# A rewritten end for a top-k attention and mixture-of-depths kernel: order, PSUM tiles, engines and the last scatter

## Chip, cores and metric

The kernel runs on one core of a Trainium2 chip. The metric is the device time of one execution in microseconds (us); lower is better. A core has five engines that the profile names PE (TensorE, matmuls; PEld is its weight load), DVE (VectorE), ACT (ScalarE), POOL (GpSimd) and SP (SyncE, here a queue of transfers). Each works through its own instructions in order and waits on semaphores for the others.

## The reference

Two blocks follow each other: top-k attention, then a mixture of depths over the result.

```python
# attention: q, k, v are (8, 8, 576, 64)
scores = scale * np.matmul(q, k.transpose(0, 1, 3, 2))
kth = np.partition(scores, -32, axis=-1)[..., -32:-31]
scores = np.where(scores >= kth, scores, -1000000000.0)
attn = softmax(scores)                       # written out in the reference
x = attn @ v                                 # -> (8, 576, 512), heads side by side
# mixture of depths: w_gate (512), w1 (512, 1024), w2 (1024, 512), capacity 128
gate = np.einsum('bsd,d->bs', x, w_gate)
out = x.copy()
for b in range(8):
    top_idx = np.argpartition(-gate[b], 128)[:128]
    xe = x[b, top_idx]
    ye = np.maximum(xe @ w1, 0.0) @ w2
    out[b, top_idx] = xe + sigmoid(gate[b, top_idx])[:, None] * ye
```

## The kernel before

A batch of 576 rows is cut into four tiles of 128 rows and a last one of 64 (`J` = 4, `NT` = 5). A unit is a tile with two heads; the last tile puts four heads in one unit. That gives 18 units a batch and N = 144 in all. One software pipeline runs over the units. A unit goes through these steps:

- `multiply` and `keep`: scores on PE into the PSUM tile `ps`, copied to SBUF as `sc` by ACT.
- `find_bound` (DVE): a bound on the kth score from maxima of seven parts.
- `what_is_below`: ACT takes the sign of score against bound (`sides`, two instructions, with a sum in `seen`), POOL multiplies score and sign into `y`.
- `kth_of` (DVE): the eight largest of `y` (`next`), the last of which is the kth score.
- `mask_of`: `less` is 1 in bf16 where a score lies below the kth. In the loop ACT takes one half and POOL the other.
- `weigh`: PE turns the scores (`turn`, `turn_last`) and adds a large negative number where `less` is set; ACT takes the exponential into `pT` and `last`.
- `values` (PE) multiplies with v into `av`; `keep_values` (ACT) copies to `xs`, `keep_sums` keeps the denominators `sums`.
- When a tile is whole, `normalise` divides (`rden` on DVE, the product `x` on POOL), and `gates` takes the dot product with w_gate on DVE (`gate`).

When a batch is whole its rows are stored from `x` by SP, and `mixture` follows in slices between the units of the next batch: each gate is counted against all others (`junk`, with the count in `rank`), the rank is compared with the slot numbers (`pick`), PE multiplies `pick` with the split parts of row number and gate (`parts`, made by `split` on POOL), an indirect transfer on POOL gathers the 128 rows `xe`, PE turns them (`xeT`), multiplies with w1 (`h_ps`, `hT`) and w2 (`y_ps`), and POOL scatters the product `gy`, adding to the rows in `out`.

All engine instructions go through `InOrder`, which keeps them in program order, so the order of the text is the order on each engine, and the profile gives line 45 for nearly all of them. [...] `ps_sc` takes four (the score tile `ps`), `ps_tr` two (`ptr`), `ps_av` one (`av`), `ps_misc` one.

After the loop (from line 1188) the end of the last batch is written out. Units N-4 to N-1 are still to be weighed. They take turns between the tiles `ptr`, `av` and, by `other_room`, the score tile, both halves of which carry the name `ps`. `closing`, a generator, holds the selection of the last batch without a trip through DRAM: `spread` turns the gates into a row on all partitions, `count` counts, `split`, five `pick`, places, gather, the multiplications, and one scatter that writes x + g y. Slices of `between`, the mixture of batch B-2, are put into it. A certificate follows: DVE reduces `least`, `seen`, `sums`, `ranks` and `others` to one flag `unsure`, and `count_unsure` puts it through PE. All engines load the flag (line 1298), and an exact general path would run if it were set.

Of the kernel before, what the change touches and what calls it, by code (L numbers as in the profile page):

```python
# [10 lines left out]
AF = mybir.ActivationFunctionType  # L11
# [8 lines left out]
CAP = 128  # L20
# [11 lines left out]
J = 4  # L32
# [16 lines left out]
def kernel(  # L49
# [38 lines left out]
        tc.tile_pool(name="dram", bufs=2, space=bass.MemoryType.DRAM)  # L88
    )
    PS = bass.MemoryType.PSUM  # L90
    ps_sc = ctx.enter_context(tc.tile_pool(name="ps_sc", bufs=1, space=PS))
    ps_tr = ctx.enter_context(tc.tile_pool(name="ps_tr", bufs=1, space=PS))
    ps_av = ctx.enter_context(tc.tile_pool(name="ps_av", bufs=1, space=PS))
    ps_misc = ctx.enter_context(tc.tile_pool(name="ps_misc", bufs=1, space=PS))


    ident = const.tile([P, P], FP32, name="ident")
# [48 lines left out]
    ranks = const.tile([P, B, NT], FP32, name="ranks")  # L146
    nc.gpsimd.memset(ranks, 0.0)

    others = const.tile([P, J], FP32, name="others")

# [34 lines left out]
    def flush():  # L187
        while late:
            late.pop(0)()
# [5 lines left out]
    def flush_pool():  # L195
        while pool_late:
            pool_late.pop(0)()
# [545 lines left out]
        )  # L743
        pool_late.append(lambda: add_rows(gy, row_i))

    def closing(b, pg, between):

        gate, rank = pg[0], ranks[:, b, :]
        gate_row = modpool.tile([P, S], FP32, name="gate_row")
        pick = modpool.tile([P, NT, CAP], BF16, name="pick")

        def spread(t0, t1):
            tr = ps_tr.tile([P, 2, J, P], FP32, name="ptr")
            n = R if t0 == J else P
            for t in range(t0, t1):
                pe.transpose(  # L760
                    tr[:, 0, t - t0, 0:n],
                    gate[0:n, t : t + 1].to_broadcast([n, P]),
                    ident[0:n, 0:n],
                )
            act.copy(
                out=gate_row[:, t0 * P : (t1 - 1) * P + n].rearrange(
                    "p (t i) -> p t i", i=n
                ),
                in_=tr[:, 0, 0 : t1 - t0, 0:n],
            )  # L770

        def count(t, among, rank):
            n = R if t == J else P
            junk = modpool.tile([P, S], FP32, name="junk", tag="scratch")
            dve.tensor_scalar(
                out=junk[0:n, among],
                in0=gate_row[0:n, among],
                scalar1=gate[0:n, t : t + 1],
                scalar2=None,
                op0=ALU.is_gt,  # L780
                op1=ALU.add,
                accum_out=rank[0:n, t : t + 1],
            )

        spread(0, J)
        yield
        for t in range(J):
            count(t, slice(0, JP), rank)
            if t == 1:
                yield  # L790
        yield
        spread(J, NT)
        split(*pg)
        for _ in range(2):
            next(between)
        for t in range(J):
            count(t, slice(JP, S), others)
        for t in range(J):
            (pool if t < 3 else dve).tensor_scalar(
                out=pick[:, t, :],  # L800
                in0=slot,
                scalar1=rank[:, t : t + 1],
                scalar2=others[:, t : t + 1],
                op0=ALU.subtract,
                op1=ALU.is_equal,
            )
        count(J, slice(0, S), rank)
        dve.tensor_scalar(
            out=pick[0:R, J, :],
            in0=slot[0:R, :],  # L810
            scalar1=rank[0:R, J:NT],
            scalar2=None,
            op0=ALU.is_equal,
        )
        ps = ps_av.tile([P, 512], FP32, name="av")[:, 0:6]
        place = stats.tile([P, 2], FP32, name="place")
        row_i = modpool.tile([P, 1], I32, name="row_i", bufs=2)
        g = modpool.tile([P, 1], FP32, name="g", bufs=2)
        multiply_places(ps, pick, pg)
        add_parts(place, ps)  # L820
        keep_rows(place, row_i, float(b * S), float((b + 1) * S - 1))
        xe = modpool.tile([P, HD], FP32, name="xe")
        fetch_rows(xe, out[0 : b + 1], row_i)
        dve.tensor_scalar_max(out=g, in0=place[:, 1:2], scalar1=-88.0)
        act.activation(g, g, AF.Exp, scale=-1.0)
        for _ in between:
            pass
        flush()
        flush_pool()
        yield  # L830
        dve.tensor_scalar_add(out=g, in0=g, scalar1=1.0)
        dve.reciprocal(out=g, in_=g)

        xeT = modpool.tile([P, NDC, CAP], FP32, name="xeT")
        ps = ps_tr.tile([P, 2, J, P], FP32, name="ptr")[:, 0, :, :]
        for dc in range(NDC):
            pe.transpose(ps[:, dc, :], xe[:, dc * P : (dc + 1) * P], ident)
        act.copy(out=xeT, in_=ps)
        yield
        hT = modpool.tile([P, NFC, CAP], FP32, name="hT")  # L840
        for f0 in range(0, NFC, 2):
            h_ps = (
                lambda: room_for_scores()[:, 0, 0, :],
                lambda: ps_av.tile([P, 512], FP32, name="av"),
                lambda: ps_misc.tile([P, 512], FP32, name="h_ps", tag="misc"),
                lambda: ps_tr.tile([P, 2, J, P], FP32, name="ptr")[:, 0, :, :].rearrange(
                    "p c i -> p (c i)"
                ),
            )[f0 // 2 % 4]()
            for i in range(2):  # L850
                multiply_h(h_ps[:, i * CAP : (i + 1) * CAP], f0 + i, xeT)
            act.activation(
                hT[:, f0 : f0 + 2, :],
                h_ps[:, 0 : 2 * CAP].rearrange("p (f i) -> p f i", f=2),
                AF.Relu,
            )
        ps = room_for_scores()[:, 0, 0, :]
        for fc in range(NFC):
            pe.matmul(
                ps, hT[:, fc, :], w2[:, fc, :], start=(fc == 0), stop=(fc == NFC - 1)  # L860
            )

        gy = modpool.tile([P, HD], FP32, name="gy")
        dve.scalar_tensor_tensor(
            out=gy, in0=ps, scalar=g[:, 0:1], in1=xe, op0=ALU.mult, op1=ALU.add
        )
        put_rows(gy, row_i)

    def multiply_places(ps, pick, pg):

        for t in range(NT):
            n = R if t == J else P
            pe.matmul(
                ps,
                pick[0:n, t, :],
                pg[1][0:n, t, :, :].rearrange("p a e -> p (a e)"),
                start=(t == 0),
                stop=(t == J),
            )

    def split(gate, parts):

        rest = modpool.tile([P, NT], FP32, name="rest")
        pool.tensor_copy(out=parts[:, :, 1, 0], in_=gate)
        pool.tensor_tensor(rest, gate, parts[:, :, 1, 0], ALU.subtract)
        pool.tensor_copy(out=parts[:, :, 1, 1], in_=rest)
        pool.tensor_tensor(rest, rest, parts[:, :, 1, 1], ALU.subtract)
        pool.tensor_copy(out=parts[:, :, 1, 2], in_=rest)
# [29 lines left out]

        put_rows(gy, row_i, compute_op=ALU.add)

    def put_rows(rows, row_i, **how):
        pool.indirect_dma_start(
            out=out.flatten_outer_dims(),
            out_offset=bass.IndirectOffsetOnAxis(ap=row_i, axis=0),
            in_=rows,
            in_offset=None,
            **how,
        )
# [256 lines left out]

    def other_room():
        ps = room_for_scores()
        return ps[:, 0, :, :].rearrange("p u (c i) -> p u c i", c=J), ps[:, 1, 0, :]  # L1190

    x, pg = of_batch[B - 1]
    between = mixtures[B - 2]
    last_out = out[B - 1]
    weighed = {}

    def weigh_unit(m):
        tr, av = other_room() if (N - m) % 2 else room_to_turn()
        weighed[m] = *weigh(scs.pop(m), tr, av, masks.pop(m)), av

    def values_unit(m):
# [9 lines left out]
        n = R if t == J else P  # L1211
        keep_sums(n, xs, sums[0:n, (B - 1) * NT + t, :])

    weigh_unit(N - 4)
    weighed[N - 4][2]()
    what_is_below(N - 1)
    mask_of(N - 3, (dve, dve))
    weigh_unit(N - 3)
    kth_of(N - 2)
    mask_of(N - 2, (act, dve))  # L1220
    values_unit(N - 4)
    weighed[N - 3][2]()
    keep_unit(N - 4, xs)
    flush()
    weigh_unit(N - 2)
    kth_of(N - 1)
    mask_of(N - 1, (act, dve))
    values_unit(N - 3)
    weighed[N - 2][2]()
    keep_unit(N - 3, xs)  # L1230
    sums_of(J - 1, xs)
    normalise(B - 1, J - 1, xs)
    store_full(last_out, x)
    weigh_unit(N - 1)
    gates(B - 1, J - 1)
    values_unit(N - 2)
    weighed[N - 1][2]()
    xs = xpool.tile([P, H, DE], FP32, name="xs")
    keep_unit(N - 2, xs)
    closed = closing(B - 1, pg, between)  # L1240
    next(closed)
    values_unit(N - 1)
    for _ in range(2):
        next(between)
    keep_unit(N - 1, xs)
    sums_of(J, xs)
    next(closed)
    normalise(B - 1, J, xs)
    store_last(last_out, x)
    next(closed)  # L1250
    gates(B - 1, J)
    next(closed)


    keep_least(B - 1, bounds.pop(B - 1)[:, :, :, 7], next8s.pop(B - 1)[:, :, :, 7])
    sure = stats.tile([P, 1], FP32, name="sure")
# [23 lines left out]
    dve.memset(ones, 1.0)  # L1280
    unsure = const.tile([1, 1], I32, name="unsure")

    def count_unsure():
        ps = ps_av.tile([P, 512], FP32, name="av")
        pe.matmul(ps[0:1, 0:1], sure, ones)
        dve.tensor_scalar(
            out=unsure,
            in0=ps[0:1, 0:1],
            scalar1=-1.0,
            scalar2=float(P + B * (S * (S - 1) // 2)),  # L1290
            op0=ALU.mult,
            op1=ALU.add,
        )

    next(closed)
    count_unsure()
    next(closed, None)
    is_unsure = nc.values_load(unsure[0:1, 0:1])  # L1298


    def general_weights(sc):
# [103 lines left out]
```

## Time and profile before

| | us |
|---|---|
| median of three runs | 826.69 (826.53 to 827.79) |
| the profiled execution, as run | 828.44 |
| its span in the profile | 826.1 |
| PE busy | 777.0 (94%) |
| DVE busy | 787.2 (95%) |
| ACT busy | 730.7 (88%) |
| POOL busy | 715.4 (87%) |
| mean granted clock of TensorE | 0.99 |

The span is what the profiler saw of one execution; the time as run holds some more around it. A busy share is an average over the whole span. The page also cuts the span into 40 slices of equal length and gives the busy share of each engine in tenths, a 9 standing for 90% or more. The loop over the units fills the span from the start to about 780 us; the end after the loop takes the rest. A trace answer lists single instructions with their start, and in brackets how long the engine had been idle before and which engine's instruction ended the wait.

### The profile page before, as it was taken

What the parts mean: (1) busy time and instruction counts of PE and PEld (TensorE: products, weight loads), DVE (VectorE), ACT (ScalarE), POOL (GpSimd) and SP (SyncE); (2) the same over time, 40 slices, a digit from 0 to 9 for tenths busy, and PEclk for the clock granted to TensorE, in tenths of its full rate; (3) what the DMA queues carried; (4) which work ended last, traced back from release to release, by engine and by line L of the source; (5) the groups of instructions that cost most, each with busy time, mean ns of one, the idle gap of its engine ahead of it and who ended that gap; (6) DMA issues with size and microseconds to landing.
All of it is one profiled execution on the core that took longest, in us unless ns stands there. A gap on an engine that the chain in (4) does not pass through costs nothing. (4 is left out here: it accounts for less than half of the span.)

```text
span 826.1 us, 28252 instructions
## 1 busy us (share of the span) xinstructions
PE 777.0 (94%) x10143; PEld 596.5 (72%) x10143; DVE 787.2 (95%) x4651; ACT 730.7 (88%) x1557; POOL 715.4 (87%) x722
## 2 busy tenths in 40 slices
PE   6888888888999999999999999999999999999976
PEld 5566666666887778877787777877787777767744
DVE  7899999999999999999999999999999999999960
ACT  4799999999999999999999999999999999879831
POOL 3799999999899999999899999999999998899831
PEclk9699999999999999999999999999999999999999
DMA  7931111521141221521223221512215102101021
GB/s 170 283 86 40 28 66 28 105 53 27 60 92 36 53 40 59 112 47 34 79 47 86 53 40 60 104 23 54 40 59 112 28 15 66 23 12 18 2 71 30
DMA packets 122133, 50.38 MB, mean 61 GB/s; under 512 B 116417, under 2 KB 116417, under 8 KB 120961
## 3 DMA queue, kind: packets, MB, share of 16 engines
q1 hardware_dynamic: 118672, 43.91, 22.0%
q0 software_dynamic: 1728, 4.20, 2.8%
q8 instruction: 82, 1.34, 0.8%
q14 instruction: 67, 0.54, 0.3%
q10 hardware_dynamic: 1584, 0.39, 0.2%
HBM read 36.93 MB, written 11.55 MB: 59 GB/s over the span
## 5 line engine op out<-in xcount | busy, mean ns | idle before, releaser
L45 POOL TENSOR_TENSOR y<-sc,sides 128x576 f32<-128x576 f32 x288 | 365.1, 1289 | 57.0 <-ACT sides L45 54.3
L45 DVE MAX8 cand<-sc 128x8 f32<-128x82 f32 (+1 forms) x2016 | 314.0, 228 | 2.7 <-ACT sc L45 2.7
L45 POOL TENSOR_SCALAR less<-sc,next 128x576 bf16<-128x576 f32 x135 | 232.5, 1722 | 12.9 <-DVE next L45 10.0
L45 PE MATMUL ptr<-out_of_reach,less 128*128 128x128 bf16 x1136 | 205.3, 220 | 19.5 <-POOL less L45 19.4
L45 ACT ACTIVATE sides<-sc,bound 128x576 bf16<-128x576 f32 x288 | 223.0, 787 | 0.0
L45 PE MATMUL ptr<-ident,sc 128*128 128x128 f32 x1136 | 217.0, 282 | 0.0
L45 DVE MAX8 next<-y 128x8 f32<-128x584 f32 x288 | 204.4, 751 | 1.7 <-POOL y L45 1.6
L45 PEld LDWEIGHTS av<-v,pT 128*64 128x64 f32 x4544 | 144.1, 137 | 66.9 <-ACT last L45 63.2
L45 PE MATMUL ps<-kT,qT 64*128 64x288 f32 (+1 forms) x1280 | 182.0, 431 | 5.2 <-ACT qT L45 5.2
L45 PEld LDWEIGHTS ptr<-ident,sc 128*128 128x128 f32 x1136 | 161.3, 142 | 29.1 <-issue 17.4
L45 ACT ACTIVATE pT<-ptr 128x1024 f32<-128x1024 f32 x142 | 145.3, 1023 | 33.2 <-PE ptr L45 32.2
L45 PE MATMUL av<-v,pT 128*64 128x65 f32 x4544 | 163.7, 224 | 9.3 <-ACT last L45 8.5
L45 ACT COPY sc<-ps 128x1152 f32<-128x1152 f32 (+1 forms) x144 | 162.2, 1126 | 3.5 <-PE ps L45 3.5
L45 PEld LDWEIGHTS <-less 128*128 128x128 bf16 x1296 | 136.1, 106 | 39.2 <-POOL less L45 25.2
L45 PEld LDWEIGHTS ps<-kT,qT 64*128 64x128 f32 (+1 forms) x1280 | 100.2, 178 | 41.5 <-issue 21.2
L45 ACT ACTIVATE less<-sc,next 128x576 bf16<-128x576 f32 x143 | 111.2, 777 | 12.7 <-DVE next L45 10.8
L45 DVE MATCH_REPLACE8 cand<-best,cand 128x21 f32<-128x21 f32 (+1 forms) x576 | 99.0, 180 | 0.0
L45 DVE MAX8 best<-cand 128x8 f32<-128x21 f32 (+1 forms) x576 | 90.5, 190 | 0.0
L45 PE MATMUL h_ps<-xeT,w 128*128 128x128 f32 x464 | 65.8, 286 | 0.0
L45 PEld LDWEIGHTS h_ps<-xeT,w 128*128 128x128 f32 x464 | 55.8, 191 | 9.2 <-issue 5.8
L45 PE MATMUL y_ps<-w,hT 128*128 128x512 f32 x112 | 60.6, 636 | 0.0
L45 ACT ACTIVATION_READ_ACCUMULATOR sides<-sc,bound 128x1 f32 x288 | 59.9, 208 | 0.0
(133 smaller groups left out, 866.4 us busy)
## 6 DMA issues: line engine op xcount, KB each, us to landing
v<-in_v_dram SPq DMA_DIRECT2D x64, 128.0 KB, 4.2
out_dram<-x SPq DMA_DIRECT2D x8, 1024.0 KB, 3.9
rows<-in_k_dram SPq DMA_DIRECT2D x56, 128.0 KB, 2.9
rows<-in_q_dram SPq DMA_DIRECT2D x56, 128.0 KB, 3.1
w<-in_moe_w_dram SPq DMA_DIRECT2D x2, 2048.0 KB
gate_row<-row_dram SPq DMA_DIRECT2D x7, 288.0 KB, 4.4
w<-in_k_dram SPq DMA_DIRECT2D x8, 128.0 KB, 3.2
last<-in_k_dram SPq DMA_DIRECT2D x8, 128.0 KB, 4.0
```

What stands on the lines that cost most here:

```text
L45: return lambda *a, **kw: self._tc.keep_in_program_order(fn(*a, **kw))
```

## The change

Nothing in the loop over the units changes but where its PSUM score tile lies: `ps_sc` is opened last and closed after the loop, and a pool `ps_end` takes its four banks for the end, as `tr2` (two banks), `av2` and `av3`. `closing` goes; its steps stand in the open at the end, in another order:

- The signs of the last unit come ahead of everything else of the end.
- Units N-3 and N-1 are weighed in `tr2` with `av2` and `av3`, units N-4 and N-2 in `ptr` with `av` as before.
- The masks of N-3, N-2 and N-1 are all made by DVE, with a sum that nothing reads (`compare`). Before, N-3's two were DVE's, and the other four were shared by ACT and DVE; none had a sum.
- The gates of tiles 0 to 2 are spread and counted against each other while the last units are weighed; those of tile 3 and of the last tile are counted when they are known, in columns of their own (`others`, now with five columns and cleared at the start).
- The last tile's `x` is made by DVE in place of POOL.
- The slots: tiles 0 and 1 by POOL, tile 2 by ACT as relu(1 - |rank - slot|), tiles 3 and 4 by DVE. Before: three by POOL, two by DVE.
- `xeT` is copied in two halves, by ACT and by DVE.
- The certificate's matmul stands between the two multiplications, and the flag is loaded ahead of the last steps of DVE and POOL.
- The product with w2 is made in two halves of 256 columns, each with its own `gy` and its own scatter, into `out` seen as rows of 256.

```diff
+    all_steps = ExitStack()
+    ps_sc = all_steps.enter_context(tc.tile_pool(name="ps_sc", bufs=1, space=PS))
...
-    others = const.tile([P, J], FP32, name="others")
+    others = const.tile([P, NT], FP32, name="others")
+    nc.gpsimd.memset(others, 0.0)
...
-    def closing(b, pg, between):
...
+    all_steps.close()
+    end = ExitStack()
+    ps_end = end.enter_context(tc.tile_pool(name="ps_end", bufs=1, space=PS))
...
+    def other_room(m):
+        tr = ps_end.tile([P, 2, J, P], FP32, name="tr2")
+        return tr, bank(ps_end, "av2" if m == N - 3 else "av3")
...
+    def compare(out, in0, scalar, op, total):
+        dve.tensor_scalar(
+            out=out, in0=in0, scalar1=scalar, scalar2=None,
+            op0=op, op1=ALU.add, accum_out=total,
+        )
...
+    what_is_below(N - 1)
     weigh_unit(N - 4)
+    rows_ps = bank(ps_end, "av3")
+    turn_gates(0, J - 1, rows_ps)
     weighed[N - 4][2]()
-    what_is_below(N - 1)
-    mask_of(N - 3, (dve, dve))
+    keep_gates(0, J - 1, rows_ps)
+    mask_both(N - 3)
     weigh_unit(N - 3)
     kth_of(N - 2)
-    mask_of(N - 2, (act, dve))
     values_unit(N - 4)
     weighed[N - 3][2]()
     keep_unit(N - 4, xs)
     flush()
+    mask_both(N - 2)
     weigh_unit(N - 2)
     kth_of(N - 1)
-    mask_of(N - 1, (act, dve))
     values_unit(N - 3)
     weighed[N - 2][2]()
     keep_unit(N - 3, xs)
     sums_of(J - 1, xs)
+    mask_both(N - 1)
     normalise(B - 1, J - 1, xs)
     store_full(last_out, x)
     weigh_unit(N - 1)
+    for t in range(2):
+        count(t, slice(0, (J - 1) * P), rank)
     gates(B - 1, J - 1)
+    count(2, slice(0, (J - 1) * P), rank)
     values_unit(N - 2)
     weighed[N - 1][2]()
     xs = xpool.tile([P, H, DE], FP32, name="xs")
     keep_unit(N - 2, xs)
-    closed = closing(B - 1, pg, between)
-    next(closed)
+    tr = ps_tr.tile([P, 2, J, P], FP32, name="ptr")[:, 0, 0, :]
+    turn_gates(J - 1, J, tr)
+    keep_gates(J - 1, J, tr)
     values_unit(N - 1)
     for _ in range(2):
         next(between)
     keep_unit(N - 1, xs)
     sums_of(J, xs)
-    next(closed)
-    normalise(B - 1, J, xs)
+    count(J - 1, slice(0, JP), rank)
+    rden = stats.tile([P, H], FP32, name="rden")
+    dve.reciprocal(out=rden[0:R, :], in_=sums[0:R, (B - 1) * NT + J, :])
+    dve.tensor_tensor(
+        x[0:R, J, :].rearrange("p (h d) -> p h d", h=H), xs[0:R, :, 0:D],
+        rden[0:R, :].unsqueeze(2).to_broadcast([R, H, D]), ALU.mult,
+    )
     store_last(last_out, x)
-    next(closed)
     gates(B - 1, J)
...
+    split(*pg)
+    count(J, slice(0, JP), rank)
+    for t in range(J - 1):
+        count(t, slice((J - 1) * P, S), others)
+    count(J - 1, slice(JP, S), others)
+    count(J, slice(JP, S), others)
+    for t in (0, 1):
+        pool.tensor_scalar(out=pick[:, t, :], in0=slot, ...)
+    whole = stats.tile([P, 1], FP32, name="whole")
+    far = modpool.tile([P, S], FP32, name="far_slot", tag="scratch")[:, 0:CAP]
+    act.activation(whole, others[:, 2:3], AF.Identity, bias=rank[:, 2:3])
+    act.activation(far, slot, AF.Abs, bias=whole, scale=-1.0)
+    act.activation(pick[:, 2, :], far, AF.Relu, bias=1.0, scale=-1.0)
+    for t in (J - 1, J):
+        dve.tensor_scalar(out=pick[0:n, t, :], in0=slot[0:n, :], ...)
...
+    for copy, half, dc in zip((act.copy, dve.tensor_copy), halves, (0, 2)):
+        copy(out=xeT[:, dc : dc + 2, :], in_=half[:, 0 : 2 * CAP]...)
...
+    for i in range(2):
+        for fc in range(NFC):
+            pe.matmul(
+                halves[i][:, 0:W], hT[:, fc, :], w2[:, fc, i * W : (i + 1) * W],
+                start=(fc == 0), stop=(fc == NFC - 1),
+            )
+    half_rows = out.rearrange("b s (e w) -> (b s e) w", w=W)
+    is_unsure = nc.values_load(unsure[0:1, 0:1])
+    for i in range(2):
+        gy = modpool.tile([P, W], FP32, name=f"gy{i}", tag=("gy", "gate_row")[i])
+        dve.scalar_tensor_tensor(
+            out=gy, in0=halves[i][:, 0:W], scalar=g[:, 0:1], in1=xe[:, columns], ...
+        )
+        put_rows(gy, half_i[:, i : i + 1], half_rows)
```

## The prediction

> **What bounds the kernel now.** The slices of the page come first: in the body all four engines are 90% busy or more, and the diff touches nothing there but the place of the score tile in PSUM and one memset. What falls is the end.
>
> ```profile
> PE   6888888888999999999999999999999999999976
> DVE  7899999999999999999999999999999999999960
> ACT  4799999999999999999999999999999999879831
> POOL 3799999999899999999899999999999998899831
> ```
>
> One slice is 20.7 us, so the change lives in the last 45 us. The page's chain of waits is no help: it holds two pieces, the last issue alone. I therefore read the timeline of each engine from 777 us and followed the releasers back by hand. Columns: start, duration (us), engine, line, operation, in brackets the idle time before and its releaser.
>
> ```profile
> 781.37 0.78 ACT L45 ACTIVATE sides<-sc,bound 128x576 bf16<-128x576 f32 x1
> ...
> 786.87 0.52 DVE L45 TENSOR_SCALAR less<-sc,next 128x576 bf16<-128x576 f32 x1
> ...
> 787.88 0.27 ACT L45 COPY xs<-ps 128x130 f32<-128x130 f32 x1
> 788.20 0.33 PE L45 MATMUL ps<-ident,sc 128*128 128x128 f32 x1 [1.33 <-ACT xs L45]
> ...
> 794.30 1.04 POOL L45 TENSOR_TENSOR x<-xs,rden 64x512 f32<-64x512 f32 x1 [4.54 <-DVE rden L45]
> 797.79 2.40 POOL L45 TENSOR_SCALAR pick<-slot,ranks,others 128x128 bf16<-128x128 f32 x3
> 800.25 0.31 PE L45 MATMUL av<-parts,pick 128*128 128x6 bf16 x3 [0.59 <-POOL pick L45]
> 801.23 1.07 POOL L45 DMA_INDIRECT xe<-out_dram,row_i  x1 [1.04 <-DVE least L45]
> 804.86 0.63 PE L45 MATMUL ptr<-ident,xe 128*128 128x128 f32 x4 [0.66 <-DMA xe<-out_dram,row_i]
> 806.16 2.05 PE L45 MATMUL ps<-xeT,w 128*128 128x128 f32 x16 [0.56 <-ACT xeT L45]
> 813.41 7.03 PE L45 MATMUL ps<-w,hT 128*128 128x512 f32 x16
> 820.55 0.75 DVE L45 SCALAR_TENSOR_TENSOR gy<-ps,g,xe 128x512 f32<-128x512 f32 x1 [14.77 <-PEq L1368]
> 821.59 1.01 POOL L45 DMA_INDIRECT out_dram<-gy,row_i  x1 [14.44 <-DVEq L1368]
> ```
>
> The reader sees one serial chain. The last unit's turn on PE (788.20) waits until ACT has emptied the tile that it shares with unit N-3. The last gate is ready at 796.45. Three slot comparisons on POOL end at 800.19; the gather lands 3.57 us after its issue; PE then runs the MLP without a gap from 806.16 to 820.44. Behind it stand gy, the scatter, its landing and 1.5 us of closing (821.59 + 3.0 landing = 824.6, span 826.1). Two more answers price what is changed: groups by form, and the DMA view of 821 to 826.5 us.
>
> ```profile
> L45 DVE TENSOR_SCALAR_CACHE_REDUCE junk<-gate_row,gate 128x576 f32<-128x576 f32 x28 | 22.1, 789 | 1.9 <-DMA gate_row<-row_dram 1.9
> ```
> ```profile
> out_dram<-gy,row_i POOLq DMA_INDIRECT x1, 3.0
> ```
>
> [...] the same mask takes 0.52 us at 786.87 with POOL idle, 1.16 at 782.81 with POOL in y, 0.98 at 779.37. The summing form takes 0.79 in 28 runs beside a busy POOL, so it doesn't show that wait. [...] the trace has one load in all (1.28 us), for Exp, Sign and Relu together; Abs isn't in it. [...]
>
> **The change, part by part.** I take durations from the rows above and place them in the changed kernel's instruction order as built; hand-over between engines is 0.03 to 0.15 us in the trace (0.29 for a POOL DMA). Times are on before's clock; everything up to 778.7 us is the same.
>
> *Signs first, own tiles, masks.* ACT runs unit N-1's signs at 778.7 instead of 781.37 (1.63 us for two). POOL's y for it follows N-2's at 780.85 and is done at 783.6, not 785.30. ACT loses two masks (2 x 0.78) and its exponentials for N-4 to N-2 follow at 780.35, 782.3 and 785.45. DVE gets all six masks, pitch 0.79 + 0.07 for the accumulator read = 0.86: N-3 779.5 to 781.25, kth N-2 (1.42) to 782.67, N-2 to 784.5, kth N-1 to 785.97, N-1 to 787.75. That is 0.36 later than before's 787.39: the masks themselves gain nothing. What gains is PE. With a tile of its own the last turn no longer waits for xs; its first half starts at 787.0, the second (0.17 a pair, five pairs) at 787.85, so it ends at 788.8 against 789.96. ACT is then idle and starts pT at 788.75 instead of 790.00. Gain here 1.25 us. The three gate transposes put ahead of N-3's turn (0.5 us) are hidden: N-3's masks end at 781.25, and PE reaches the values of N-4 at 782.45 as before (782.50). Uncovered they would cost 0.5.
>
> *Known gates early.* Counts of gates 0 to 2 over 384 columns (0.66 each by the line through 0.79 for 512 and 0.33 for 64) sit in DVE's gap before and after gate 3; the count of gate 3 fits ahead of the sums. Values of N-1 run at 790.45 (before 791.78), sums end at 792.65 (793.99).
>
> *x on DVE.* [...] against 1.04 on POOL, and DVE no longer sits in a count when it arrives. Gate 4 at 794.45 against 796.45: gain 2.0. The added waits on old stores of x have long been met. SP's last store now waits for DVE, is issued 1.6 us earlier and lands ahead of the gather; SP has nothing else queued.
>
> *Slots.* Before, POOL's split (1.3) and three picks (0.805 each) decide: 800.19. Now POOL does two, 795.85 to 797.45. DVE counts: gate 4 to 795.3, three over 192 columns (0.46) to 796.67, two over 64 to 797.33, then picks to 798.0. ACT's slot takes three operations and shares the scratch buffer with the counts, so its second waits for the last count, 797.38, though its data is there at 796.7; behind it on ACT stand pick, g, gy and xeT. With 0.40 each [...] it ends at 798.2 and is last. Bounds for it: 0.27 (a 128-column exponential) to 0.5 each, or 797.95 to 798.4. Places end 798.55 against 800.56; gather 799.22 against 801.23; gain 2.0. It lands at 802.8; PE's remaining y_ps (3.70) ends by 802.15.
>
> *xeT in halves.* Before: 804.86 to 806.16 = 1.30. Now ACT copies 256 columns (0.38) behind two transposes while DVE copies the rest (0.42): the MLP starts 0.87 after the first transpose, at 803.7. Gain 2.45.
>
> *MLP, certificate, y in halves.* h takes 7.25 as before. The certificate's matmul moves ahead of y, a new wait of PE on DVE's checks with all of y behind it: they run 4.1 us from 803.95, to 808.1, and h ends at 810.95; hidden with 2.9 to spare. y becomes 16 products of 256 columns: [...] (a record of 128 columns takes 112 ns, of 512 439), plus 0.1; ends 818.2, gain 2.25. gy of 256 columns is 0.48 instead of 0.75, so the last scatter is issued at 819.05 against 821.59: gain 2.55. Half of its bytes may save up to 0.3 more; bound from below 0. The register load on each engine moves ahead of gy and scatter; it waits for a flag ready at 811.2, y's first half is there at 814.55: free.
>
> *The one wait that is added on the path.* The second scatter waits for the first to land, since both write out; only the branch stands behind it. The first is issued at 815.35 and lands at 818.35 with before's 3.0. The second is ready at 819.05: 0.7 us of cover.
>
> The memset of others at the start (0.1 on POOL) lies beside loads; at worst 0.1.
>
> Sum: 2.55 + 0.15 = 2.7 us. The profiled execution has a span of 826.1 and took 828.44, 2.3 around it and 1.75 above the median of the runs; I take the difference from the median: 826.69 - 2.7 = **824.0 us**. Errors of up to 0.1 at each of ten hand-overs give 823.0 to 825.0 for this case.
>
> **Rivals.**
> The halves collide. If the first scatter lands like the adding one of 805 us (5.1) instead of 3.0, the second is issued at 815.35 + 5.1 + 0.3 = 820.75, 1.7 late: 825.7. For: the rows are shorter and as many. Against: 3.0 measured for the plain write with twice the bytes.
>
> Part of the front is lost again: the ACT slot at its upper bound, DVE picks stretched by POOL (0.35 and 0.40 were), hand-overs longer, together 1.2 us: 825.2.
>
> Slower: DVE's masks become the bound. Six stand in series before the last turn. The summing form with bf16 output has no row. If it needed POOL's 1.72 us for the same mask, six cost 6 x 0.86 = 5.2 more, less the 2.7 gained: 829.2. It evens out at 1.31 each and decides from 1.58. Against: 789 ns for the same operation with f32 output, over 28 runs. From below it could fall to the 0.52 of the mask without a sum, 6 x 0.34 = 2 us on DVE, of which POOL's y (783.6) lets through under 1; so the low end is 822.8.
>
> That the change doesn't do what it says is excluded by the built order: the last turn waits for DVE's masks alone.
>
> **The numbers.** About 0.2% (1.65 us) is what a measurement of this kernel can tell from no change. Forecast 0.76, all of it faster by over 0.2%; colliding halves 0.11, no change; lost front 0.07, 0.02 of it faster and 0.05 no change; masks 0.06, slower. So faster 0.78, same 0.16, slower 0.06. The range reaches from 822.8 over the lost front and colliding halves to 826.0.
>
> **What would show it.** In the profile after: six CACHE_REDUCE masks near 0.8; PE's last turn released by DVE less, ended 1.2 earlier; gate 4 at 794.5; places released by ACT pick at 798.3; gather issue at 799.2; MLP from 803.7; last scatter at 819.1, 0.5 or more after the first has landed. Wrong would be masks over 1.3, a last scatter released by the first one's landing, or a gather at 801 or later.

## The result and the profile after

The changed kernel takes 823.41 us by the median of 11 runs (821.96 to 825.44); the kernel before took 826.65 beside it (824.87 to 827.79). The ratio is 0.9964, with a 95% interval of 0.9953 to 0.9974: faster by 3.2 us, with the whole interval below 1. Six runs of the same kernel later gave a ratio of 0.9966 (0.9953 to 0.9978).

The profiled execution took 823.15 us and has a span of 820.6. Against the span before, 826.1, that is 5.5 us less, more than the medians say. Part of it is not the change's: the same instruction at the fork, the search for unit N-3's kth score (`MAX8 next` of DVE), starts at 775.60 in this profile and at 778.03 in that of before, and the code up to there is the same. In 14 profiles of this study it starts anywhere from 775.32 to 778.84 (the last section shows why). From here on, "after the fork" counts from the start of that instruction in the same profile, which takes this difference out. From the fork to the end of the span it is 45.00 us here and 44.74 in a second profile of the same kernel, against 48.07 before: 3.1 to 3.3 us less, which agrees with the medians. To set an absolute time of the profile after on before's clock, add 2.43.

The timeline of the changed kernel, in single instructions, for the same steps as shown of before (start, duration, engine, line, operation, in brackets idle time and releaser):

```profile
776.15 0.77 ACT L45 ACTIVATE sides<-sc,bound 128x576 bf16<-128x576 f32 x1
777.65 0.81 DVE L45 TENSOR_SCALAR_CACHE_REDUCE less<-sc,next 128x576 bf16<-128x576 f32 x1
785.67 1.03 ACT L45 ACTIVATE pT<-tr 128x1024 f32<-128x1024 f32 x1 [1.00 <-PE tr L45]
789.77 0.68 DVE L45 TENSOR_TENSOR x<-xs,rden 64x512 f32<-64x512 f32 x1
792.62 1.58 POOL L45 TENSOR_SCALAR pick<-slot,ranks,others 128x128 bf16<-128x128 f32 x2
794.15 0.40 ACT L45 ACTIVATE far_slot<-slot,whole 128x128 f32<-128x128 f32 x1 [0.40 <-DVE junk L45]
794.95 0.31 PE L45 MATMUL av<-parts,pick 128*128 128x6 bf16 x3 [0.51 <-ACT pick L45]
795.93 1.07 POOL L45 DMA_INDIRECT xe<-out_dram,row_i  x1 [1.73 <-DVE g L45]
799.39 0.66 PE L45 MATMUL av<-ident,xe 128*128 128x128 f32 x4 [0.50 <-DMA xe<-out_dram,row_i]
800.29 2.05 PE L45 MATMUL ptr<-xeT,w 128*128 128x128 f32 x16 [0.24 <-ACT xeT L45]
807.75 7.17 PE L45 MATMUL av<-w,hT 128*128 128x256 f32 x32
812.35 1.01 POOL L45 DMA_INDIRECT out_dram<-gy,half_i  x1 [10.58 <-DVE gy L45]
815.73 0.96 POOL L45 DMA_INDIRECT out_dram<-gy,half_i  x1 [2.37 <-POOLq L1430]
```

The chain has the same links as before. Most are shorter; from the last gate to the gather (4.76 us, before 4.79) and from the MLP, the first product with w1, to the last scatter (15.44, before 15.43) it takes as long. The masks with a sum take 0.80 us, and one starts 0.72 after the other. The exponential of the last unit starts 10.07 after the fork, before 11.97. ScalarE's slot ends last of the five, after its wait for the counts (`junk`). The second scatter is issued 40.13 after the fork, before 43.56.

What is absent matters as much. Here is TensorE in stretches of the front of the end: length, busy time with instructions, granted clock, DMA. First the kernel before:

```profile
778.00:782.00 4.00, 3.52 (x39) 1.00 0.00 0
782.00:786.00 4.00, 4.00 (x77) 1.00 0.02 4
786.00:790.00 4.00, 2.67 (x47) 1.00 0.00 0
```

and the changed kernel:

```profile
776.00:780.00 4.00, 4.00 (x51) 1.00 0.00 0
780.00:784.00 4.00, 4.00 (x90) 1.00 0.01 4
784.00:788.00 4.00, 4.00 (x82) 1.00 0.31 131
788.00:790.00 2.00, 2.00 (x24) 1.00 0.66 262
```

Before, PE idled 1.8 us here (0.48 for a mask, 1.33 for the copy of xs). After, it never waits: the front is filled with TensorE's own work.

### The profile page after: what moved, and what is told of

Its sections match the earlier page's. It is cut to its first block, busy times and chain, and to the rows that moved or that the text cites. A ratio compares the mean times of both kernels' runs of the same rounds, so it can differ in the third digit from the quotient of the medians.

```text
span 820.6 us, 28306 instructions
## 1 busy us (share of the span) xinstructions
PE 775.1 (94%) x10159; PEld 598.2 (73%) x10159; DVE 788.8 (96%) x4666; ACT 729.7 (89%) x1559; POOL 714.9 (87%) x722
## 3 DMA queue, kind: packets, MB, share of 16 engines
q8 instruction: 82, 1.34, 0.7%
## 5 line engine op out<-in xcount | busy, mean ns | idle before, releaser
L45 PEld LDWEIGHTS av<-v,pT 128*64 128x64 f32 x4608 | 146.1, 137 | 66.9 <-ACT last L45 63.0
L45 ACT ACTIVATE pT<-ptr 128x1024 f32<-128x1024 f32 x142 | 145.2, 1023 | 34.2 <-PE ptr L45 33.3
L45 PE MATMUL av<-v,pT 128*64 128x65 f32 x4608 | 166.0, 224 | 9.0 <-ACT last L45 8.2
```

Of the source, the lines that this page charges most:

```text
L45: return lambda *a, **kw: self._tc.keep_in_program_order(fn(*a, **kw))
```

## The experiments

All are edits of the changed kernel. Except where a ratio is given they ran once, and are judged in the trace, after the fork. The table holds the start of each step; "pT, N-1" is the last unit's exponential, "MLP" the first product of the gathered rows with w1, "sums" the end of the last tile's sums, "gate" that of the last gate.

| kernel | pT, N-1 | sums | gate | gather issued | MLP | last scatter |
|---|---|---|---|---|---|---|
| before | 11.97 | 15.96 | 18.41 | 23.20 | 28.13 | 43.56 |
| changed | 10.07 | 13.90 | 15.57 | 20.33 | 24.69 | 40.13 |
| changed, again | 10.06 | 13.90 | 15.56 | 20.32 | 24.71 | 40.15 |
| plain masks | 10.54 | 14.37 | 16.03 | 20.79 | 25.18 | 40.61 |
| signs late | 11.17 | 15.01 | 16.68 | 21.44 | 25.84 | 41.27 |
| shared room | 10.68 | 14.34 | 16.00 | 20.76 | 25.40 | 40.83 |
| all three | 11.44 | 15.10 | 16.77 | 21.53 | 26.17 | 41.60 |
| gates late | 9.75 | 13.91 | 15.57 | 21.51 | 27.21 | 42.64 |
| gates late, filled | 9.75 | 13.91 | 15.57 | 21.51 | 26.20 | 42.60 |
| x on POOL | 10.07 | 13.90 | 15.97 | 20.73 | 25.20 | 40.63 |
| own far slots | 10.07 | 13.90 | 15.57 | 19.96 | 24.30 | 39.73 |
| y whole | 10.05 | 13.88 | 15.55 | 20.31 | 24.75 | 40.49 |
| one copy of xeT | 10.07 | 13.90 | 15.57 | 20.33 | 25.22 | 40.66 |
| two further edits | 9.71 | 13.54 | 15.21 | 20.22 | 24.62 | 40.05 |

The repetition of the changed kernel agrees within 0.02 us at each step, so differences of 0.1 us mean something up to the issue of the gather. Its landing varies by some 0.1 us.

**The front: masks, signs, room, and all three.** The theory formed on the trace was that TensorE is the bound there and the other engines only have to be in time; the rival, that signs, y, masks and turns are one serial chain.

```diff
-            compare(masks[m][:, a, :], scs[m][:, a, :], kth, ALU.is_lt, some)
+            dve.tensor_scalar(out=masks[m][:, a, :], in0=scs[m][:, a, :],
+                              scalar1=kth, scalar2=None, op0=ALU.is_lt)
```

> The masks of units N-3, N-2 and N-1 on VectorE are made without the sum, in the form of before. Theory A (TensorE is continuously busy from unit N-3's masks to unit N-1's first turns, and the masks only have to be in time): the plain masks last 0.7 to 1.0 us each where GpSimd works beside them, the last turn of N-1 moves by at most 0.5 us, the end becomes 0.2 to 0.5 us later than in the changed kernel, counted from a common point at the fork. Theory B (the summing form carries the gain of the front): the masks fall back to before's 0.98 us, six of them are 0.25 us later each, and the end comes 1.5 us later or more.

Measured: 0.47 later at the sums. TensorE gets 0.33 us behind at a mask of N-3 (the trace shows 0.17 of it as idle time) and 0.13 more at a mask of N-2. The first plain mask of N-3 takes 1.53 us and the first of N-2 1.44, both begun while GpSimd is in y; the other four take 0.50 or 0.51 each. The summing ones take 0.80 throughout. Theory A holds. The sum buys an even pace, not a fast one.

```diff
-    what_is_below(N - 1)
     weigh_unit(N - 4)
...
     keep_gates(0, J - 1, rows_ps)
+    what_is_below(N - 1)
```

> Unit N-1's signs are issued after the exponentials of unit N-4, as before; all else as in the changed kernel. Theory A (TensorE is the bound in the front): GpSimd's y of N-1 comes about 1.1 us later, the first mask of N-1 becomes ready at about the time at which TensorE needs it, and the end comes about 0.45 us later (0 to 0.6). Theory B (signs, y, masks, turns are one serial chain): the whole 1.1 us or more is seen at the end.

Measured: 1.11 later at the sums, so theory A fails, and so does its arithmetic: the signs come 3.1 us later and the y of N-1 is done 2.0 later, not 1.1, because ScalarE's copy of the gates and an exponential stand ahead of the signs there. Of the 2.0, 0.9 was slack; the rest becomes a wait of TensorE, which the waits of this kernel between 777 and 790 us show as the only one (total, times, longest):

```profile
PE tr L45 <- DVE less L45: 0.9, 1, 0.9
```

So a PE without a gap did not mean that the serial chain was far from binding; it lay 0.9 us behind.

The next edit puts the turns and the values of a unit into one PSUM tile again (the "room"), as before:

```diff
-        tr = ps_end.tile([P, 2, J, P], FP32, name="tr2")
-        return tr, bank(ps_end, "av2" if m == N - 3 else "av3")
+        both = ps_end.tile([P, 3, 512], FP32, name="tr2")
+        tr = both[:, 0:2, :].rearrange("p u (c i) -> p u c i", c=J)
+        return tr, both[:, 2, :]
```

> The turns of a unit in the end and its values lie again in one tile of three banks, of which there are two, as before; the other new tiles stay. Theory A (TensorE is the bound in the front, and now reaches N-1 late anyway): the turns of N-1 wait for ScalarE's copy of xs of N-3 for about 0.45 us, and the end comes as much later (0.2 to 0.7). Theory B (the shared room alone made before's wait): the turns of N-1 wait 1.3 us again and the end comes 1.3 us later. Theory C: the copy is done in time, and nothing changes (within 0.15 us).

Measured: 0.44 later at the sums, theory A. The timeline of this kernel has before's wait again, at 0.37 instead of 1.33 us, and a second one, later, that my edit made: half of the turned `xe` had to go to the bank of `y_ps`, which `gy` still reads. That is 0.28 of the 0.71 at the MLP.

```profile
786.03 0.33 PE L45 MATMUL tr<-ident,sc 128*128 128x128 f32 x1 [0.37 <-ACT xs L45]
801.65 0.44 PE L45 MATMUL h_ps<-ident,xe 128*128 128x128 f32 x2 [0.78 <-ACT gy L45]
```

The three edits together:

> The three edits of the front are undone together: signs of N-1 after the exponentials of N-4, masks without the sum, turns and values in one shared tile; all else as in the changed kernel. Alone they cost 1.1, 0.47 and 0.43 us at the sums of the last tile. Theory A (three limits that lie close together, each of them binding in its turn): together they cost 1.9 to 2.2 us, about their sum and about what the front gained. Theory B (they hide each other): about 1.1 to 1.4 us, the greatest of them alone and little more.

Measured: 1.20 later at the sums, theory B. The costs alone (0.47 + 1.11 + 0.44 = 2.02) do not add: the limits lie side by side, and undoing one uses the slack of the others. With all three undone the front still ends 0.86 earlier than before. Its timeline holds TensorE's three waits:

```profile
780.89 0.23 PE L45 MATMUL tr<-out_of_reach,less 128*128 128x128 bf16 x1 [0.16 <-DVE less L45]
787.17 0.33 PE L45 MATMUL tr<-ident,sc 128*128 128x128 f32 x1 [0.37 <-ACT xs L45]
787.77 0.23 PE L45 MATMUL tr<-out_of_reach,less 128*128 128x128 bf16 x1 [0.26 <-DVE less L45]
```

The copy of xs is awaited 0.37 us instead of 1.33. Signs, room and mask form are before's here; what remains of the change in the front are two masks less on ScalarE and the early gates. Before, ScalarE made a mask of 0.78 us for N-2 and one for N-1 ahead of that copy, and the copy started 9.85 after the fork; here 8.88. I read the 0.86 as the two masks; no run put them back alone.

**Gates early.**

```diff
-    rows_ps = bank(ps_end, "av3")
-    turn_gates(0, J - 1, rows_ps)
...
-    turn_gates(J - 1, J, tr)
-    keep_gates(J - 1, J, tr)
+    turn_gates(0, J, tr)
+    keep_gates(0, J, tr)
...
     gates(B - 1, J)
+    for t in (2, 3):
+        count(t, slice(0, JP), rank)
```

> The first three columns of known gates are turned together with the fourth, after the values of N-2, and the counts of the first four columns follow there, over all 512 known gates at once: two of them ahead of the normalisation of x, two after the last gate. Theory A (the early ranks are worth what VectorE no longer does after the last gate): the places come 1.3 to 1.6 us later, less at most 0.1 us that TensorE gains in the front by not turning gates there, and the end 1.2 to 1.6 us later. Theory B (TensorE's three turns of gates in the front cost what the counts bring): the front ends 0.5 us earlier, and the end comes at most 0.8 us later.

Measured: the gather is issued 1.18 later (theory A, just under its range), but the MLP starts 2.52 later, which neither theory has. The three turns do cost TensorE in the front: without them pT of N-1 starts 0.32 earlier; ahead of the last values they cost the same. The rest is the clock. TensorE waited 1.45 us for the first slot (GpSimd's, as the weight load in front of that product shows; the expectation of the next run lays it to ScalarE), then stood idle 0.60 and 0.24 between the slots, and then the stretches show this (length, busy, clock, DMA):

```profile
797.00:798.00 1.00, 1.00 (x3) 0.50 0.03 8
798.00:799.00 1.00, 1.00 (x3) 0.50 0.51 61
```

At half the clock the eight remaining products of `y_ps` took 5.40 us instead of 3.70, and TensorE came to the gathered rows after they had landed. The next run fills the wait:

```diff
     keep_gates(J, NT, tr)
-    for _ in range(2):
+    for _ in range(4):
         next(between)
```

> As the run with the gates turned late, but TensorE is given two more pieces of y of batch 6's mixture (0.94 us each) ahead of the products with the slots, where it waited 1.45 us for ScalarE; behind the slots two pieces fewer are left. In the run before, the granted clock was 0.50 from 797.3 to 801 us, and the first product of the MLP came 2.5 us later, with the gather issued only 1.2 us later. Theory A (the idle 1.45 us brought the clock down): the clock stays at 1.00, and the MLP starts 1.2 to 1.4 us later than in the changed kernel. Theory B (the clock fell by chance, or for another reason): with a fallen clock it starts 1.3 us or more later; a full clock alone would not tell chance from the idle time, but a fallen clock here excludes theory A.

Measured: the clock is 1.00 from 791 to 802 us, where it had fallen. But with two pieces fewer behind the slots TensorE waits 2.29 us for the gather, and the clock falls at the end of that wait:

```profile
803.13 1.12 PE L45 MATMUL av<-ident,xe 128*128 128x128 f32 x4 [2.29 <-DMA xe<-out_dram,row_i]
```
```profile
803.00:804.00 1.00, 0.87 (x4) 0.50 0.00 0
804.00:805.00 1.00, 0.96 (x5) 0.50 0.00 0
```

The MLP starts 1.51 later, outside theory A's 1.2 to 1.4, and its first products run at half speed, so the last scatter is as late as without the filling (2.47). I had not foreseen that the filling opens the wait behind it, so my rule that a fallen clock excludes theory A does not apply as written. What the pair shows: the fall moved with the idle time. What stays open is how much idle time it takes.

**x, slots, xeT.** Three single edits behind the sums:

```diff
-    dve.tensor_tensor(x[0:R, J, :]..., xs..., rden..., ALU.mult)
+    normalise(B - 1, J, xs)
```

> The last tile's x is divided by its sums on GpSimd, as before, in place of VectorE. Theory A (the product stands alone on the path from the sums to the last gate, and VectorE is the faster engine for it): x takes about 1.1 us in place of 0.68, and gate 4, the places, and the end come about 0.45 us later. Theory B (the last gate waits for something else as well, such as the store's queue): within 0.15 us of the changed kernel.

```diff
-    far = modpool.tile([P, S], FP32, name="far_slot", tag="scratch")[:, 0:CAP]
+    far = modpool.tile([P, CAP], FP32, name="far_slot")
```

> The tile of far slots has a buffer of its own, and no longer shares one with the counts' scratch. Theory A (ScalarE's far slots wait for VectorE's last count only through that buffer): the far slots are written ahead of the last count, ScalarE's pick starts as soon as the ranks are there, and the places and the end come 0.25 to 0.4 us earlier. Theory B (GpSimd's two picks end last or just as late): the places come at most 0.1 us earlier.

```diff
-    for copy, half, dc in zip((act.copy, dve.tensor_copy), halves, (0, 2)):
-        copy(out=xeT[:, dc : dc + 2, :], in_=half...)
+    act.copy(out=xeT, in_=halves.rearrange("p (c i) -> p c i", c=NDC))
```

> The four turned pieces of xe lie in one bank again and are copied by ScalarE in one instruction, as before. Theory A: from the last turn to the first product of the MLP it takes 1.3 us in place of 0.9, and the end comes 0.4 us later. Theory B (the weights or the queue of TensorE hold the first product): no change within 0.1 us.

Measured, theory A in all three: x on GpSimd takes 1.04 us, the gate comes 0.40 later; far slots in a buffer of their own start without the wait, and bring the gather 0.37 earlier; one copy of xeT needs 1.33 us from the first turn to the MLP in place of 0.90. What no run undid is the move of the third slot from GpSimd to ScalarE and the new place of the certificate's product.

**y whole.**

```diff
-    for i in range(2):
-        for fc in range(NFC):
-            pe.matmul(halves[i][:, 0:W], hT[:, fc, :], w2[:, fc, i * W : (i + 1) * W], ...)
+    for fc in range(NFC):
+        pe.matmul(whole_y, hT[:, fc, :], w2[:, fc, :], ...)
...
-        put_rows(gy, half_i[:, i : i + 1], half_rows)
+    put_rows(gy, row_i)
```

> The last product y is made in one piece of 512 columns, with one product by the gate and one scatter. Theory A (the halves hide the first half's gy and scatter, and pay for it with twice as many products): y ends about 0.14 us earlier, gy takes about 0.75 us in place of 0.48, the scatter is issued 0.1 to 0.2 us later and lands in about 3.0 us; the end comes 0.1 to 0.3 us later. Theory B (the second scatter waits for the first one's landing, and this costs what the halves bring): the end comes as early as with halves, or up to 0.4 us earlier.

Measured: the scatter is issued 0.36 later and lands 3.0 us after its issue, but the span ends 45.08 after the fork, against 45.00 and 44.74 in the two profiles of the changed kernel. That is 0.08 to 0.34 later, which does not tell theory A (0.1 to 0.3 later) from theory B (as early, or earlier): with halves the last landing alone takes anything from 2.6 to 3.0 us. So no gain of the halves at the end of the span is shown. Theory B's reason does fail, since the first scatter had landed in time. What takes back the 0.36, if anything does, is the closing behind the last landing, 1.6 us here and 2.0 with halves. SP's waits from the last scatter on, first of the changed kernel, then of this one:

```profile
SPq L1462 <- PEq L1462: 1.2, 2, 0.9
```
```profile
SPq L1449 <- PEq L1449: 0.8, 2, 0.5
```

In all 12 profiles with two scatters the closing is 1.9 to 2.0 us, in the two with one 1.5 and 1.6. What TensorE's sequencer does there the trace does not show.

**A version with two further edits**, and the changed kernel beside it:

```diff
-        B - 2: (5, 6, 6, 7, 7, 7, 9, 9, 11, 12, 13, 14, 15, 16, 16, 17, 17),
+        B - 2: (5, 6, 6, 7, 7, 7, 9, 9, 11, 12, 13, 14, 15, 16, 16, 17),
...
     values_unit(N - 1)
-    for _ in range(2):
+    for _ in range(3):
         next(between)
...
     sums_of(J, xs)
+    flush()
...
-    far = modpool.tile([P, S], FP32, name="far_slot", tag="scratch")[:, 0:CAP]
+    far = modpool.tile([P, CAP], FP32, name="far_slot")
```

> Two edits on the changed kernel: the far slots have a buffer of their own, and the last piece of the first product of batch 6's mixture (0.93 us of TensorE) moves from the last step of the loop to behind the values of N-1, where TensorE waits 0.74 us for the last gate. Theory A (TensorE and the chain of signs, y and masks are both nearly the bound in the front): TensorE reaches the turns of N-3 0.9 us earlier and waits there for VectorE's masks, which bring 0.3 to 0.4 of it to the end; with 0.4 from the far slots the last scatter comes 0.7 to 0.8 us earlier from the fork, and the time is 822.65 (0.991 of the kernel before, 0.7 us under the changed one). Theory B (the moved piece delays the turn of the last gate, or the masks hold all of the front): only the 0.4 of the far slots is seen.

> The changed kernel once more, unaltered, beside the version with two further edits: 823.4 by its median, and from the last scatter to the end of the span 4.5 to 4.9 us. If the tail of 2 us behind the last landing belongs to the change, it is 4.8 or more again; if it differs from execution to execution, it lies anywhere in 4.5 to 4.9.

Measured: 822.48 us, a ratio of 0.9952 (0.9939 to 0.9966), against 823.37 and 0.9966 (0.9953 to 0.9978) for the changed kernel. The intervals overlap, and in the trace the last scatter is issued only 0.08 earlier, so no gain over the changed kernel is shown. That 822.65 had been named is luck: the step behind it, 0.7 to 0.8 at the last scatter, did not come. The front does bring its 0.36. It is lost to a wait that I made: the first product with w2 now waits for ScalarE to write the last part of hT, which it does not read.

```profile
790.19 1.98 PE L45 MATMUL y_ps<-w,hT 128*128 128x512 f32 x4 [0.47 <-ACT hT L45]
```

Behind it the turn of the last gate starts at 792.11, 0.47 later after the fork than in the changed kernel, and takes the far slots' gain with it. The far slots alone (39.73) are the better version by the trace; they were timed once, at 823.03, so a gain in time is not shown. In the repeated kernel it is 4.59 us from the last scatter to the end of the span, where the first profile had 4.87: the last landing takes 2.6 us instead of 2.9 and the closing is 1.99 instead of 1.97. So the landing varies, the closing stays.

## Why the prediction was right, and where its steps were not

Faster, with a chance of 0.78, and 824.0 us were named; 823.41 came. The steps, as gains over before after the fork:

| step | predicted | measured |
|---|---|---|
| exponential of N-1 | 1.25 | 1.90 |
| sums | 1.34 | 2.06 |
| last gate | 2.0 | 2.84 |
| gather issued | 2.0 | 2.87 |
| MLP | 2.45 | 3.44 |
| end of y | 2.25 | 3.09 |
| last scatter | 2.55 | 3.43 |
| end, by the medians | 2.7 | 3.24 |

**The mis-sized term is the masks.** I added the accumulator's read of 0.07 to 0.79 us and took a pitch of 0.86. The recorded 0.80 already overlaps the read (0.08 us, at 777.65) and the start of the next (777.65, the first at 776.93): the pitch is 0.72. Six masks make 0.8 us of it, and the last mask ends at 784.08 (786.51 on before's clock), not 787.75. Of these 1.24 us TensorE's own work let 0.65 through to the exponential. From there to the last scatter every step keeps its predicted size within 0.15 us. The named time came nearer than its parts by luck: at the last scatter the gain forecast was 0.88 too small, and a closing 0.4 to 0.5 longer, which was not foreseen either, took half of that back.

**A mechanism was named wrongly beside it.** "The last turn waits for DVE's masks alone" is true of the order as built and not of the time: PE had no wait at all, and the release by "DVE less" that was to show it did not appear. The three gate turns, costed at nothing because masks would cover them, lie on TensorE's path (0.32). And the gain of the own tile was laid to the shared room alone; with the room shared again the wait was 0.37, not 1.33, since ScalarE's copy then starts 8.56 after the fork instead of 9.85.

**Readings that do not hold.** The 0.98 us given for a mask at 779.37 is the mean of two, 1.54 and 0.51, so a plain mask has no such duration. The scatter's 3.0 us, taken as one landing, are for the most part not data: the bulk of it passes between 823.1 and 824.1 us, so some 1.5 us pass before it and only 0.5 behind it until the landing. And not all engines are at 90% in the body: nine slices of PE alone show an 8. Two prices come out of the traces as they were used. ScalarE's 0.40 us for a slot is the 777 ns of a mask of 576 columns less 448 x 0.84, with 0.84 ns a column by the exponentials of before (1023 ns for 1024 columns, 273 for 128). A record of 256 columns, 221 ns by the line through before's 112 for 128 columns and 439 for 512, was 224 (7.17 us for 32).

**Right as stated:** x is faster on VectorE (the author's estimate, which no trace of before showed; measured 684 ns, against 1.04 us on GpSimd); the slot's 0.40 and its wait for the scratch buffer (undone, 0.37 come back); no table load is added with Abs (an estimate too; the trace after has one load in all, 1.28 us, as before); xeT at 0.90 instead of 0.87; the certificate hidden (its last check ends at 804.6, its matmul runs at 807.63). The second scatter's cover came out as worked out. From the DMA view, the landings of the first and the second:

```profile
out_dram<-gy,half_i POOLq DMA_INDIRECT x1, 2.4
```
```profile
out_dram<-gy,half_i POOLq DMA_INDIRECT x1, 2.9
```

The first lands at 814.75; the second is issued at 815.73, with the 0.29 of hand-over 0.69 us of cover against 0.7.

**Missed:** the closing, taken as unchanged at 1.5, grew to 2.0. It takes back what the halves gain at the issue (0.36). The product in halves is 0.35 longer in all, where 0.2 was taken.

**The rivals.** Colliding halves: no, the plain scatter lands in half the 5.1 us. Lost front: no, ScalarE took 0.40 and 0.31, VectorE's picks 0.34 and 0.33. Masks as the bound: not at 0.80 us; but their chain lay only 0.9 behind TensorE, so the rival's place was right and its price wrong.

## What to carry to other kernels

Where several engines are near their limit in one stage, price each edit by what the others let through: the parts of this front cost 0.4 to 1.1 us to undo alone and 1.2 together, and an engine without a gap can have another 0.9 us behind it. A pitch is read from two starts, not from a duration plus the read that follows. And a scatter in halves has to be followed to the end of the span, not to its issue.

## What the runs showed of the hardware

**The start.** TensorE's granted clock stood at 0.50 for a stretch near the start of every profile, and the stretches come in steps of 3.4 us: 6.8, 10.2 or 13.7 us (in two, six and six of the 14 profiles). One line each, of before and after, from the stretches of equal length:

```profile
32.00:36.00 4.00, 4.00 (x48) 0.67 1.04 411
```
```profile
32.00:36.00 4.00, 4.00 (x62) 0.92 1.03 406
```

The fork starts at 775.3 to 776.4, 775.6 to 777.2 and 777.9 to 778.8 us with them, whatever the kernel; the two profiles shown here had 13.7 and 10.2. With 13.7 before's fork, at 778.03, lies among those of the changed kernel's edits, so no difference of the loop itself is seen. Comparing two spans without a common point would have credited 2.4 us of it to the change.

**The clock inside the kernel.** With the gates turned late the clock fell to 0.50 for about 3.4 us, with a longest gap of 1.45 us, two short products and a gap of 0.60 behind it; with the wait filled it fell again, with one gap of 2.29. Gaps of 0.74, 0.60, 0.51 and 0.50 us within 9 us, in the changed kernel, did not bring the clock down: it stayed at 1.00. Whether the longest gap or the share of idle time decides, no run here tells.

**Plain masks beside GpSimd.** In the kernel before and in the runs with plain masks, six masks were begun while GpSimd was in an instruction of y. Each ended 0.31 to 0.32 us after that instruction did, however long that took (1.16 to 1.54 us in all), and a mask begun without such a neighbour took 0.50 to 0.52. It holds the other way too: an instruction of y begun during a plain mask took 1.50 to 1.54 us in place of 1.28. In these traces, then, each holds up the other: the mask by up to 1.0 us, y by 0.2 to 0.3. With the sum neither is held up: the masks take 0.80 us, and two instructions of y 2.53.
